# Combining C and B before the transposition, with wider products and a new instruction order, in a state-space convolution kernel

## The chip, the cores and the metric

The kernel runs on one core of one Trainium2 chip. The metric is the device time of one execution in microseconds. The core has five engines, each with its own instruction queue that runs in order: PE (TensorE), DVE (VectorE), ACT (ScalarE), POOL (GpSimd) and SP, which here only issues DMAs. Engines wait for each other through semaphores.

## The reference, cut to what matters

The input `x` has 2048 rows of 512 columns (bf16). Two branches are computed and mixed row by row with a gate `g`:

```
g = sigmoid((x * gate_w).sum(-1))
# branch a: a convolution along the 2048 rows, one kernel K per column d
dt    = exp(log_dt)                                  # 512
P     = exp(dt * A * l)                              # A complex, 512 x 128 states, l = 0..2047
K     = real(sum_n C[d,n] * P[d,n,l] * dt * B[d,n])  # C and B complex
a     = causal_conv(x, K) + x * Dskip                # by FFT in the reference
# branch b: the two rows with the largest x @ w_r go through a gated MLP and are added back
b     = x + scatter(silu(xs @ w_gate) * (xs @ w_up) @ w_down * sigmoid(r))
out   = g * a + (1 - g) * b
```

For this change what counts is `C * dt * B`, a complex product of 512 x 128 numbers that the kernel needs transposed (states on the partitions), and the products of spectra by which the convolution is done.

## The kernel before, in words

**How the order is set.** The kernel records operations (`P.op`) with what they read and write. Nothing is scheduled at run time: a string `ORDER` lists all operations in one sequence, three characters for each, and a string `SECOND` says for operations that two engines could do (`EV`, `SCL`, `LIN` and some others: ACT or DVE) which one does it. `P.fixed` deals the sequence out to the engines' queues, and `P.emit` adds the waits. A wait is needed for results of other engines and, on DVE and ACT, also for results of the engine itself. So a change of any operation comes with a new `ORDER` and `SECOND`, and every queue may be rearranged, SP's queue of DMAs included.

**Helpers and their lines.** Most DVE products come from `TT` (L483, a tensor_tensor), scalings from `TS` (L487) and `SCL` (L502 on either engine), PSUM evictions from `EV` (L498 on either engine), exponentials, sines and tanh on ACT from `AC` (L494). DMAs come from `DMA` (L505).

**Opening.** `PRM` receives A, C and B (real and imaginary part, 512 x 128 each); `CB` receives constants (`c_bf`: first the identity, later the rest). 28 matmuls on dummy data (L617) fill PE while it waits. `ptr` (L628) transposes the six parameter matrices, 24 blocks of 128 x 128, into PSUM. `dtp` spreads log_dt over all partitions and ACT takes its exponential, `DTB`. DVE then forms, with rows put into the order that the tables need: `AL` = dt * Re A, `TMP[0]` = dt * Im A, `TMP[1]` and `TMP[2]` (scaled and rounded, L648), `B16` (L651: the angle in 16 bits), `PBR` = dt * B, `CM1` and `CM2` (C times the two parts of B), and `WW` = C * dt * B.

**Tables.** `exps1` and `exps2` are 26 exponentials of `AL` on ACT. `trig` scales `B16` by a lag (`SCL`, L502), takes the sine, adds a quarter turn (L694) and takes the sine again. `tab1` and `tab2` multiply these into tables `TP` (lags in steps of 8) and `R` (`r00` to `r31`: `WW` times powers), for two halves of the states' columns, h = 0 and 1. Exponentials and sines need different function tables on ACT; a change of table is an `ACT_TABLE_LOAD` (L255).

**Forward, kernel and spectra.** `forward` (L900) transforms the input, in two blocks of 1024 rows and four frequency tiles, with matrices `F` from `c_fwd`; `EV` puts the result into `X`. `kgen` (L917) multiplies tables to give the convolution kernel `KA`; `sel` (L933, L945) picks rows of it for half 0, and for half 1 twenty small DMAs do (`tap`, "AR<-AR" among the DMA issues), into `KC`. `sel3` (L966) picks rows for eight output rows that rounding puts at block edges ("edge rows"). `kspec` (L986, L991) transforms `KC` into spectra `KK`.

**Products and inverse.** `products` multiplies `X` with `KK` on DVE, for half h and block blk; block 1 also needs block 0's input times a second spectrum. `inverse` adds up, in four PSUM banks, the skipped input and the edge rows (L1038, L1039) and the inverse transform (L1051, in groups of 8 or 4 matmuls), evicts with the gate (L1059) and stores to `out`. Block 1 is done ahead of block 0.

**Routing.** Eight DMA transposes of `x` (L762), 64 small matmuls (L771) for gate and routing logits, a search for the two largest, and the MLP (L812, L835, L851). `xed` (L820) picks input rows for the edge rows, out of four tiles of `U` (the input in SBUF). Sixteen scalings of `U` (L880) prepare the mix.

Of the kernel before, what the change touches and what calls it, by code (L numbers as in the profile page):

```python
# [373 lines left out]
ETB = sorted({tok(s)[0] for _, _, src in EROWS for s in src})  # L374
ECOL = 384
# [3 lines left out]
def small_mats():  # L379
    eye = np.eye(128)  # L380
    sgn = np.diag(np.where(np.arange(128) % 2 == 0, 1.0, -1.0))
    xs = np.zeros((128, len(ETB), EW))
    ek = np.zeros((128, 4, 2, EW))
    oh = np.zeros((NE, 16 * 128))
    for r, (t, k, src) in enumerate(EROWS):
        for s in src:
            tb, p = tok(s)
            xs[p, ETB.index(tb), 32 + r] = 1.0
# [4 lines left out]
    return np.concatenate([eye, sgn, -sgn, xs.reshape(128, -1), ek.reshape(128, -1)], 1), oh  # L393
# [3 lines left out]
    "00100300p00q00r00200000700o01401500601700501801c01b01p00402201e00h01d01601i01y01f01k01v01g00g01901q01j01h01x01a00802301u03u04w01n01o03t02s00a04x03v00s"  # L397
    "00t00u00v02002402d01r04303s04404200w00x00y00z01002b01s01t00c02604500901101201l01301w02102702q05903w03x03z04603y02t04704805b04z04y01m05805a04902g04005c"
    "00b02j04f05005105204a04104b05d05f02502m02i05e02u05g05h05302902o02r05502n05402p02v04n01z04e02w02l04c02a00e03304m05s03404d00i02k03502c05t03602f02e04p037"
    "03802h04g05600f02805v04o04q03903a04j05u03b03i05700d04h05w04t04i04r04s04k03d05i05k03j07807907a04l05j05l00n07l03o07s07j07b07c05y00l04u05m07r07i03e03f07t"  # L400
    "07k07m00j07e07h07q07d07u06004v07n05x05z06105n05p07g03g07o05o05q07v06207w03k03l09s06307f07p09t09h06e06f09r07x03m05r06h03n03q09u09v06g09i06506407y06609w"
    "06i06709x09j07z08108006j08309k06k06m0680820ae08508409l06906l06n08609m09o06b06a06c06d09n08908b0ad08a08e08f0a408h06z09y08c0a308808706y07003p06o08d0a1071"
    "07200k08g08i08j0ac09p0a20a508k08l08m08o08n08q0ab09z0af0a808p06q08s08r0a609q0a70a006p0a900m06r0am0al0ag08t0aa0an08u0ao07408w0b80ai0ah0ay0ax0az0ap0b508v"
    "0aj0b708y08x0aw0900b60ak08z0920au0aq0ar0at03r02x07306s06u0b00b306w0av0b90b106t0ba0bb0bc0as0be0bh0bd0b20b40bf0760bg0bj0bi0750bl0910bk0bu09306v0br09d0bq"
# [19 lines left out]
def bass_gated_mix__ssm_conv_s4__moe_arch_mod__prompt_kernel(nc, A_u, A_A_re, A_A_im, A_B_re, A_B_im, A_C_re, A_C_im, A_log_dt, A_Dskip,  # L424
# [22 lines left out]
    with ExitStack() as es:  # L447
# [640 lines left out]
        for qd in range(2):  # L1088
            products(0, (qd,), (1,), pset=qd)
# [57 lines left out]
```

## Time and profile before

| What | us |
|---|---|
| Median of 3 runs | 169.58 (169.01 to 169.94) |
| Profiled execution, its own time | 168.23 |
| Its span, first to last instruction | 166.4 |
| DVE busy | 152.9 |
| PE busy | 148.1 |
| ACT busy | 117.2 |
| Mean granted clock of TensorE | 0.969 |

The profile is of one execution. A matmul's busy time counts from its start to its modelled end, and matmuls overlap, so PE's busy time is not its work; start-to-start distances are. On DVE and ACT an instruction that waits for nothing starts a little before the end of the one ahead of it, so durations add up to slightly more than the time. A line of a view names the helper's line (L483 for nearly every product), so products are told apart by their shapes. "AR" is the one large SBUF tensor in which all buffers lie, "ps" is PSUM.

### The profile page before, as it was taken

The page shows a single profiled execution, that of the slowest core. Times are in us where ns is not written, and L with a number is a line of the kernel's source. Part 1 is how long each engine was busy: PE and PEld are TensorE (multiplying, and loading weights), DVE is VectorE, ACT ScalarE, POOL GpSimd, SP SyncE. Part 2 cuts the span into 40 slices and gives each one's busy share as a digit, 9 for nine tenths or more (in the row PEclk, how much of TensorE's full clock was granted, in tenths as well). Part 3 has the DMA queues.
Part 4 walks back from the last instruction along what each step waited for, and adds up shares of the span by engine and source line. Part 5 has one row for each costly group of instructions (what it writes and reads, how often), then busy time and mean ns, then how long its engine had stood idle before and what let it go on. Part 6 is the DMA issues. An engine that isn't in the chain of part 4 may idle for free.

```text
span 166.4 us, 3916 instructions
## 1 busy us (share of the span) xinstructions
PE 148.1 (89%) x1644; PEld 101.7 (61%) x1644; DVE 152.9 (92%) x255; ACT 117.2 (70%) x197; POOL 2.8 (2%) x7
## 2 busy tenths in 40 slices
PE   5999959999999998997489999968989999989980
PEld 1644415456364348692257799837857888878860
DVE  1699998899999998999999999999999999999970
ACT  3499999799999999999744777992043658408022
POOL 2000000000000000000000004000000000000000
PEclk9999987999999999999858999999999999999999
DMA  4999998996000000000995502941020000130505
GB/s 151 218 341 203 146 241 290 415 398 267 4 0 0 0 4 0 4 0 7 330 353 196 190 7 61 378 123 26 13 61 8 0 0 0 35 95 0 158 4 160
DMA packets 22584, 20.33 MB, mean 122 GB/s; under 512 B 12187, under 2 KB 19102, under 8 KB 22438
## 3 DMA queue, kind: packets, MB, share of 16 engines
q1 hardware_dynamic: 22276, 19.81, 39.7%
q8 instruction: 13, 0.21, 0.5%
q10 hardware_dynamic: 290, 0.26, 0.5%
q14 instruction: 5, 0.04, 0.1%
HBM read 15.54 MB, written 2.10 MB: 106 GB/s over the span
## 4 chain that ended last, share of the span: by engine, by line
DVE 52%; ACT 28%; PE 9%; issue 6%; DMA 2%; SPq 0%; DVEq 0%
DVE AR L483 44%; ACT AR L494 13%; ACT AR L498 7%; ACT AR L502 4%; PE ps L900 3%; ACT AR L694 3%; DVE AR L498 2%; PE ps L1051 2%; PE ps L628 2%; DVE AR L502 2%; DMA AR<-c_bf 2%; DVE AR L880 1%; PE ps L917 1%; PE ps L771 1%; DVE AR L1059 1%
## 5 line engine op out<-in xcount | busy, mean ns | idle before, releaser
L483 DVE TENSOR_TENSOR AR<-AR 128x1024 bf16<-128x1024 bf16 (+8 forms) x151 | 119.9, 839 | 1.3
L498 ACT ACTIVATE AR<-ps 128x512 bf16<-128x512 f32 (+7 forms) x71 | 45.0, 667 | 17.9 <-PE ps L986 10.2
L900 PE MATMUL ps<-AR 128*128 128x512 bf16 x192 | 45.5, 390 | 2.4 <-DVE AR L498 2.1
L494 ACT ACTIVATE AR<-AR 128x512 bf16<-128x512 f32 (+4 forms) x56 | 41.4, 791 | 2.6 <-DVE AR L483 2.2
L900 PEld LDWEIGHTS ps<-AR 128*128 128x128 bf16 x192 | 18.1, 100 | 25.4 <-DVE AR L498 2.6
L1051 PE MATMUL ps<-AR 128*128 128x256 bf16 x256 | 30.4, 273 | 1.3 <-DVE AR L483 1.3
L1051 PEld LDWEIGHTS ps<-AR 128*128 128x128 bf16 x256 | 24.8, 98 | 5.1 <-DVE AR L483 1.9
L1059 ACT ACTIVATE AR<-ps,AR 128x256 bf16<-128x256 f32 x25 | 10.8, 474 | 21.9 <-PE ps L1051 21.7
L986 PE MATMUL ps<-AR 128*128 128x256 bf16 x160 | 21.0, 282 | 0.3 <-issue 0.3
L917 PEld LDWEIGHTS ps<-AR 128*128 128x128 bf16 x512 | 18.8, 98 | 2.1 <-ACT AR L498 0.7
L917 PE MATMUL ps<-AR 128*128 128x84 bf16 (+1 forms) x512 | 19.4, 199 | 0.5 <-ACT AR L498 0.4
L986 PEld LDWEIGHTS ps<-AR 128*128 128x128 bf16 x160 | 15.5, 101 | 4.5 <-issue 0.7
L502 DVE TENSOR_SCALAR AR<-AR 128x256 int32<-128x256 f32 (+1 forms) x39 | 11.4, 325 | 0.6 <-ACT AR L494 0.6
L502 ACT ACTIVATE AR<-AR 128x256 int32<-128x256 f32 (+1 forms) x25 | 10.0, 437 | 0.0
L617 PE MATMUL ps<-AR 128*128 128x512 bf16 x28 | 8.3, 462 | 1.5 <-DVE AR L612 1.5
L1038 PE MATMUL ps<-AR 128*128 128x256 bf16 x32 | 7.7, 274 | 2.1 <-DVE AR L498 1.4
L1039 PE MATMUL ps<-AR 128*128 128x256 bf16 x32 | 7.6, 273 | 0.0
L483 DVE TENSOR_TENSOR AR<-AR,ps 128x256 f32<-128x256 bf16 (+2 forms) x6 | 3.4, 627 | 4.1 <-PE ps L628 4.1
L617 PEld LDWEIGHTS ps<-AR 128*128 128x128 bf16 x28 | 3.0, 112 | 5.4 <-issue 1.9
L991 PE MATMUL ps<-AR 128*128 128x512 bf16 x16 | 5.6, 380 | 0.1
L694 DVE TENSOR_SCALAR AR<-AR 128x1024 int32<-128x1024 int32 (+1 forms) x9 | 5.7, 629 | 0.0
L1038 PEld LDWEIGHTS ps<-AR 128*128 128x128 bf16 x32 | 3.1, 97 | 3.6 <-DVE AR L498 1.5
(66 smaller groups left out, 81.6 us busy)
## 6 DMA issues: line engine op xcount, KB each, us to landing
AR<-c_ksp SPq DMA_DIRECT2D x5, 512.0 KB, 5.5
AR<-c_inv SPq DMA_DIRECT2D x1, 2048.0 KB, 8.0
out_dram<-AR SPq DMA_DIRECT2D x16, 128.0 KB, 2.2
AR<-in_B_w_gate_dram SPq DMA_DIRECT2D x1, 1792.0 KB, 12.8
AR<-in_B_w_up_dram SPq DMA_DIRECT2D x2, 896.0 KB, 10.9
AR<-c_fwd SPq DMA_DIRECT2D x3, 512.0 KB, 6.9
AR<-in_A_u_dram SPq DMA_DIRECT2D x2, 512.0 KB, 5.3
AR<-in_A_u_dram SPq DMA_DIRECT2D x1, 1024.0 KB, 7.7
```

Of the source, the lines that this page charges most:

```text
L483: return P.op(DVE, lambda h: h.tensor_tensor(out=o, in0=a, in1=b, op=op), rd, wr, cost=tt_cost(o, a, b), **k)
L494: return P.op(ACT, lambda h: h.activation(out=o, in_=a, func=func, scale=scale, bias=bias), rd, wr, cost=0.185 + nel(o) * 0.833e-3 + (0.09 ...
L498: return P.op((ACT, DVE), (lambda h: h.activation(out=o, in_=a, func=ACTF.Copy), lambda h: h.tensor_copy(o, a)), rd, wr, cost=(0.185 + n * ...
L502: return P.op((ACT, DVE), (lambda h: h.activation(out=o, in_=a, func=ACTF.Copy, scale=c), lambda h: h.tensor_scalar(out=o, in0=a, scalar1= ...
L617: last = h.matmul(fwp[1](0, 128, k * 512, (1, D)), DUM(0, 128, 0, (1, 128)), DUM(0, 128, 0, (1, D)), start=True, stop=True)
L694: P.op((DVE, ACT), (lambda hh: hh.tensor_scalar(out=w, in0=w, scalar1=16384.0, scalar2=None, op0=ALU.add), lambda hh: hh.activation(out=w, ...
L900: last = h.matmul(o, w, U2(0, 128, st * D, (1, D)) if pm else U(0, 128, (blk * 8 + st * 2 + par) * D, (1, D)), start=(pm + par + st == 0), ...
L917: last = hh.matmul(pb(0, 128, (g - b0) * W4 + o, (1, n)), TP[h][1 - i // 2](0, 128, g * 128, (1, 128)), r[i](0, 128, g * n, (1, n)), start ...
L986: last = hh.matmul(pb(0, 128, n * 256, (1, 256)), KP[u](0, 128, (tau + n) * 128, (1, 128)), KC[h](0, 128, jg * 256, (1, 256)), start=(k == ...
L1038: hh.matmul(pb(0, 128, e * 256, (1, 256)), IDN(0, (1, 128)), U(0, 128, tb[e] * D + h * HC, (1, HC)), start=(e == 0), stop=False)
L1051: last = hh.matmul(pb(0, 128, e * 256, (1, 256)), G(0, 128, ((par * 2 + part) * 4 + ft) * 512 + (2 * t2 + e) * 128, (1, 128)), X(0, 128, h ...
L1059: P.op((ACT, DVE), (lambda hh, o=o, i_=i_, g_=g_: hh.activation(out=o, in_=i_, func=ACTF.Copy, scale=g_), lambda hh, o=o, i_=i_, g_=g_: hh ...
```

## The change

1. **Opening.** C is multiplied with both parts of B ahead of the transposition, packed and in bf16 (`PAB`, two products of 1024). `pwr` then transposes and adds up in one: for each of eight blocks two matmuls against the identity, the second with a negated identity (`NID`) where the complex product needs a minus, summed in PSUM (`psw`). `WW` is then one product with dt. A is transposed by matmuls against an identity whose columns are read in the tables' order and whose result is written in that order (`ptr`: runs of four floats at steps of 16), so that `AL` is one plain product and `TMP[1]` comes out of one scalar_tensor_tensor; `TMP[0]`, `PBR`, `CM1` and `CM2` are gone.
2. **Products.** For half 0, block 1, the first products are still made by pairs of frequency tiles; all that follow are done for the four tiles at once.
3. **Edge rows.** Six rows of the input are loaded by two small DMAs into `XSR`, and `xed` is one matmul on six rows.
4. **Coefficient DMAs (`tap`).** Every other one is issued from ACT.
5. **Stores by bank.** A store covers the two row tiles of one PSUM bank instead of the two parities of one row tile; there are still 16.
6. **A new `ORDER` and `SECOND`.** All 26 exponentials now stand ahead of the first sine on ACT. On SP the order of the opening loads, and of the transposes among them, is another; the rest of `c_bf` goes out ahead of the gate weights.

The diff, cut to its core (shortened expressions end in `..`):

```diff
@@ opening @@
-        pps = [misb[0], misb[1], kgb[0]]
-        for q in range(3):
+        idp = lambda b, *c: b(0, 128, *c, (64, 2), (1, 16), (16, 4))
+        pto = lambda b, c, k: b(0, 128, c + 4 * k, (HC, 2), (16, 16), (1, 4))
+        psa = [kgp[0], kgp[1]]
+        for q in range(2):
             def ptr(h, q=q):
-                for i in range(2):
-                    for k in range(4):
-                        last = h.transpose(pps[q](..), PRM(..), IDN(0, (1, 128)))
+                for k in range(4):
+                    last = h.matmul(pto(psa[q], 0, k), PRM(..), idp(CB, 0), start=True, stop=True)
+        for q in range(2):
+            TT(PAB(0, 128, q * 1024, (D, 2), (1, D)), PRM(0, 128, 2 * D, ..), PRM(0, 128, (4 + q) * D, ..), ALU.mult, ..)
+        for part in range(2):
+            def pwr(h, part=part):
+                for k in range(4):
+                    h.matmul(pto(psw, part * D, k), PAB(..), idp(CB, 0), start=True, stop=False)
+                    last = h.matmul(pto(psw, part * D, k), PAB(..), idp(CB, 0) if part else idp(NID, 0), start=False, stop=True)
...
-        for h_ in range(2):
-            TT(prd(AL, 0, h_), nat(DTB, 0, h_), tra(pps[0], 0, h_), ALU.mult, ..)
-        for h_ in range(2):
-            TT(prd(TMP[0], 0, h_), nat(DTB, 0, h_), tra(pps[0], D, h_), ALU.mult, ..)
+        TT(f512(AL), f512(DTB), psa[0](0, 128, 0, (1, D)), ALU.mult, ..)
-        LIN(f512(TMP[1]), f512(TMP[0]), [TMP[0]], [TMP[1]], scale=-c16)
+        STT(f512(TMP[1]), psa[1](0, 128, 0, (1, D)), -c16, f512(DTB), ALU.mult, ALU.mult, ..)
...
-        TT(PBR(..), DTB(..), pps[2](..), ALU.mult, ..)
-        TT(c2(CM1), pps[1](..), PBR(..), ALU.mult, ..)
-        TT(c2(CM2), pps[1](..), PBR(..), ALU.mult, ..)
-        for h_ in range(2):
-            TT(prd(WW, 0, h_), tra(CM1, 0, h_), tra(CM2, D, h_), ALU.subtract, ..)
-            TT(prd(WW, D, h_), tra(CM1, D, h_), tra(CM2, 0, h_), ALU.add, ..)
+        TT(WW(0, 128, 0, (D, 2), (1, D)), DTB(0, 128, 0, (0, 2), (1, D)), psw(..), ALU.mult, ..)
@@ edge rows @@
+            for t0 in (0, BLK):
+                DMA([(XSR(ESRC.index(t0), len(ts), 0, (1, D)), dr(A_u, t0 * D, ..))], [], [(XSR, t0)], 4096)
-                for i, tb in enumerate(ETB):
-                    last = h.matmul(xe(0, EW, 0, (1, D)), CB(..), U(0, 128, tb * D, (1, D)), ..)
+                return h.matmul(xe(0, EW, 0, (1, D)), CB(0, len(ESRC), ECOL, (1, EW)), XSR(0, len(ESRC), 0, (1, D)), ..)
@@ tap @@
-                    DMA(.., 60000 * nu, prio=1e5, each=0.6)
+                    DMA(.., 60000 * nu, prio=1e5, each=0.6, eng=(SP, ACT)[c4 % 2])
@@ products @@
+            if blks == (1,) and len(fts) == 4:
+                for qd in qds:
+                    xq = X(0, 128, h * 8192 + 4096 + 512 * qd, (2048, 2), (1024, 2), (1, 512))
+                    for P_, part in ((PA, 0), (PBb, 1)):
+                        kq = KK[h](0, 128, part * 2048 + 512 * qd, (0, 2), (1024, 2), (1, 512))
+                        TT(P_(0, 128, 512 * qd, (2048, 2), (1024, 2), (1, 512)), xq, kq, MUL, ..)
             for blk in blks:
-                for P_, part in ((PA, 0), (PBb, 1)):
+                for P_, part in ((PA, 0), (PBb, 1)) if blk == 0 or len(fts) < 4 else ():
                     TT(v4(P_), xv(blk), kv(0, part), MUL, ..)
@@ inverse @@
-                for st in range(4):
-                    tb = blk * 8 + st * 2
-                    DMA([(dr(out, (1024 * blk + 256 * st) * D + h * HC, (2 * D, 128), (D, 2), (1, HC)), U(..))], ..)
+                for t2 in range(2):
+                    for par in range(2):
+                        tb = tbs(t2, par)
+                        DMA([(dr(out, (1024 * blk + 512 * t2 + par) * D + h * HC, (2 * D, 128), (256 * D, 2), (1, HC)), U(..))], ..)
@@ calls @@
-        for qd in range(2):
-            products(0, (qd,), (1,), pset=qd)
+        products(0, (0, 1), (1,))
```

More of the change, by code (lines that the diff above doesn't have):

```diff
@@ L373 @@
 NE = len(EROWS)
-ETB = sorted({tok(s)[0] for _, _, src in EROWS for s in src})
+ESRC = sorted({s for _, _, src in EROWS for s in src})
 ECOL = 384
@@ L399 @@
[L399 to L402, printed above, removed]
```

104 lines of the change are left out of this document (55 added, 49 removed).

## The prediction

> **What bounds the kernel now.** I read first the page's busy times, then the windows by stage, the groups of VectorE by shape, the chain of waits, and the timeline of the opening and of the coefficient DMAs.
>
> The page and the windows (columns: stretch, length, busy us and instructions of PE, PEld, DVE, ACT, POOL, clock, DMA share, GB/s):
>
> ```profile
> PE 148.1 (89%) x1644; PEld 101.7 (61%) x1644; DVE 152.9 (92%) x255; ACT 117.2 (70%) x197; POOL 2.8 (2%) x7
> ```
> ```profile
> 5.57:31.00 25.43, 23.36 (x159) 11.41 (x160) 24.21 (x47) 22.85 (x39) 0.00 (x0) 0.93 1.05 256
> 31.00:80.00 49.00, 45.93 (x578) 26.95 (x575) 48.19 (x97) 48.85 (x74) 0.00 (x0) 1.00 0.22 80
> ...
> 120.30:159.00 38.70, 36.38 (x317) 29.93 (x314) 38.01 (x49) 17.55 (x37) 0.00 (x0) 1.00 0.13 39
> 159.00:166.40 7.40, 3.23 (x28) 2.66 (x28) 2.08 (x5) 1.90 (x4) 0.00 (x0) 1.00 0.31 90
> ```
>
> From its first product at 5.57 us to 159 VectorE has hardly a hole. From 31 to 80 ScalarE is full as well (48.85 of 49.00): there both set the pace together. After 80 ScalarE has half its time free and VectorE alone carries the chain. The last 7.40 us are a tail: 28 matmuls of the inverse, evictions, the last store.
>
> The prices, from the groups by shape (busy us, mean ns | idle before):
>
> ```profile
> L483 DVE TENSOR_TENSOR AR<-AR 128x2048 bf16<-128x2048 bf16 x48 | 57.5, 1220 | 0.4
> L483 DVE TENSOR_TENSOR AR<-AR 128x1024 bf16<-128x1024 bf16 x44 | 29.2, 687 | 0.4
> L483 DVE TENSOR_TENSOR AR<-AR 128x4096 bf16<-128x4096 bf16 x2 | 4.5, 2285 | 0.0
> L483 DVE TENSOR_TENSOR AR<-ps,AR 128x1024 f32<-128x1024 bf16 x2 | 2.5, 1228 | 0.0
> L483 DVE TENSOR_TENSOR AR<-AR 128x256 bf16<-128x256 f32 x4 | 2.3, 606 | 0.0
> L483 DVE TENSOR_TENSOR AR<-AR,ps 128x256 f32<-128x256 bf16 x4 | 2.1, 591 | 4.1 <-PE ps L628 4.1
> L651 DVE SCALAR_TENSOR_TENSOR AR<-AR 128x512 f32<-128x512 f32 x1 | 0.7, 693 | 0.0
> ```
>
> Doubling 1024 elements to 2048 adds 533 ns, so the fixed part is about 0.15 us. The chain shows what follows a product: 1.24 us and 0.02 of "issue" where the next one reads its result,
>
> ```profile
> 131.30 1.24 DVE AR L483
> 132.54 0.02 issue
> 132.56 1.24 DVE AR L483
> ```
>
> while an independent one starts about 0.085 us before the end of the last (four take 4.63 us in the chain, not 4.88). A wait of VectorE for itself thus costs 0.12 us.
>
> **The change, part by part.** Counts come from the two instruction orders.
>
> *Opening arithmetic, VectorE.* Gone: four 128x256 out of PSUM (591 ns), one and two of 1024 (1223, 1228), four of 256 from float (606), one L648 (429): 8.90 us, less 12 overlaps of 0.085, 7.88. New: AL and TMP[1], 512 floats each (priced as L651, 0.69), WW, 1024 out of PSUM (1.22), two of 1024 (0.687), a negated identity (0.19, between the 172 ns and 290 ns of nearby shapes): 4.17 less 0.51, 3.66. Net **-4.2**.
>
> *Half 0, block 1.* Twelve of 2048 and eight of 1024 become eight of 2048 and four of 4096: 20.14 to 18.90 us, and 8 instructions fewer give back 0.68 of overlap: **-0.6**.
>
> *Waits for itself.* 81 of VectorE's operations wait for an earlier one of its own, 65 after: 16 x 0.12 = **-1.9**.
>
> *Handed to ScalarE by the new order.* Two evictions of 1024 (1.22 and 0.68), three of 256 (0.48), two scalings of U (0.34), three small argument scalings go over; two L694 (0.69) come back for a 0.42: **-3.2** on VectorE, +3.7 on ScalarE.
>
> VectorE's queue: -9.9 us in all, 5.3 of it before its last product of the second half's table (92.9 us now) and 4.6 behind that. ScalarE: -2.6, because all exponentials now stand ahead of the sines (two L255 table loads of 1283 ns gone), +3.7, and ten coefficient DMAs.
>
> What of it lies on the path, stage by stage.
>
> Up to the last sine (now 78.9 us) ScalarE is as full as VectorE. Its queue up to there shrinks by 1.6 us (two loads -2.6, small waits -0.3, moved work +1.3). AL comes out of one instruction instead of two (0.69 for 1.10), less 0.1 because it now waits for the exponential of DTB (-0.3 before the first exponential on ScalarE), and the 1.0 us that the first L255 waited for VectorE's L502 goes with VectorE's shorter queue. So **-2.9**; VectorE's 5.3 allows it. The 13 us of VectorE behind the last sine are the same instructions.
>
> Behind 92.9, VectorE alone: -4.6. But something new is late. In PE's new order the first L986 group of half 1 stands behind the last block 1 group of the inverse. From the last product that this group needs: two inverse groups (8 x 0.109 each), two L1038/L1039 groups (4 x 0.109), one L986 group (8 x 0.109) and 0.16 to the result are 3.6 us, and VectorE has 1.22 + 0.48 + 0.27 us queued meanwhile: a hole of some 2 us, where VectorE now has its wide products of block 0. So **-2.6**.
>
> Tail: 20 matmuls instead of 28 wait for the very last product: 8 x 0.109 = **-0.9**. The last store still follows its last eviction, so storing by bank gives nothing more.
>
> Sum -6.4, before the parts that the trace doesn't price:
>
> - *Matmuls with spread rows* (24 of 128 columns at `ptr` and `pwr`, operand and result in steps, for 24 transposes at 107 ns). Low end: packed and at full clock (L1051 stands 109 apart for 256 columns, so 55 for 128), 24 x -0.052 = -1.2 us. High end from L966: with its operand in steps, eight of 64 columns took 1.14 us at half clock (127 ns start to start), with it packed 0.41 at full clock (29 ns, so 58 at half): 2.2 times. 24 x 0.107 x 1.2 is +3.1 us. Most of them stand among L900 groups that wait for loads anyway, and PE was as slow here before; I take +0.5. The Trainium skill, "PSUM — Partial Sum Buffer", Specifications, says that any non-contiguous access pattern slows matmuls significantly. It gives no factor, and no run here shows a matmul that writes in steps; what it would do is the first rival.
> - *Loads.* The order on SP is new. The second frequency tile of c_fwd (512 KB) goes out behind two transposes of U (1.2 to 3.6 us each on SP), some 3 to 4 us later than now; the first tile and U go out earlier, which gains nothing, since ScalarE is busy with exponentials until 19 us. By the bytes ahead of it and the page's GB/s row it lands at 14.7 us, with the 6.9 of its row at 16 to 17; PE is through with the first tile at about 15. Each us beyond is at most one us of ScalarE's queue, where the forward evictions stand between the sines. Between 0 and +2, I take +0.4. c_bf's rest now goes ahead of the gate weights, not behind them (12.2 us now), so the edge rows (one L820 matmul for four) that now stand ahead of L812 on PE should not stop it; if it did land at 12.2, PE, and with it the forward groups, would stand for 1.7 us.
> - *Coefficient DMAs.* SP issues the 20 in 14.2 us, 0.65 apart; ten on ScalarE are 6.5 us in the queue that also evicts. From 93 to 118.3 ScalarE is busy 16.9 of 25.3, so 8.4 cover them; an eviction behind one is up to 0.65 late. 0 to +2, I take +0.4. That they land sooner saves nothing: the last lands at 118.6 now, its reader starts at 125.2.
>
> In all **-5.1 us**. The profiled execution took 168.23 (span 166.4 and 1.8 around it), 0.8% under the median of 169.58; it would take 163.1, and the median 164.5.
>
> **The rivals.**
>
> *Spread rows are dear (slower).* The result of `ptr` and `pwr` goes to PSUM in runs of four floats, 64 bytes apart; no row shows a matmul that writes so. The chain is: AL, TMP[1] and WW wait for these, and PE's forward groups queue behind `pwr`, whose evictions ScalarE takes in order. It decides from 6.4 / 24 + 0.107 = 0.37 us for each; at 0.5 it is +9.4 against -6.4, 171 to 173 us. Against it: L966's 127 ns for 64 columns make 0.25 for 128. For it speaks the sentence of the Trainium skill above.
>
> *ScalarE and PE eat the second half.* Ten DMAs and the evictions taken over delay L986's results, the hole is 4 us and not 2: 167.2. For it: VectorE waits for 16 evictions of half 1 one by one. Against: ScalarE's 17.55 busy of 38.70 behind 120.
>
> *VectorE's cut comes through whole.* No new hole, and loads on time: -9.9 + 2 is 161.5. Against: ScalarE's full 49 us.
>
> *It evens out.* The saved instructions were under cover of ScalarE up to 80 and of PE behind it (36.38 of 38.70): 169.6.
>
> **How the numbers follow.** Forecast 0.57, ScalarE and PE 0.20, whole cut 0.08, evens out 0.05, spread rows 0.10. A measurement of this kernel can tell about 0.5% from no change, so faster 0.85, same 0.05, slower 0.10. The range leaves out the spread rows, the evening out and half of the whole cut, 0.19 together: 161.6 to 168.4.
>
> **What would show it.** VectorE some 143 us busy with 232 instructions; two table loads; the last sine at about 76 us; the last L483 of the second table at 90; a new hole of VectorE near 120, ended by PE's L983 group; 20 matmuls behind the last product. It would be wrong if `ptr` and `pwr` matmuls stand over 0.3 us apart, if PE's forward groups wait past 18 us for c_fwd, or if VectorE has over 8 us of holes from 5.6 to its last product.

## The result, and the profile after

The changed kernel takes 167.41 us (median of six runs, 167.04 to 168.25) against 169.33 of the kernel before in the same runs: ratio 0.990, 95% interval 0.986 to 0.994. The forecast was 164.5 (161.6 to 168.4). The direction was right; of 5.1 us forecast, 1.9 came. The profiled execution took 167.29 us with a span of 165.7, against 168.23 and 166.4; the one before was a fast one of its kernel, so the two profiles differ by 0.9 us and their spans by 0.7, and it is these 0.7 us that the accounting below takes apart.

Executions of one kernel differ in TensorE's granted clock (0.957 to 0.969 in these six), and the time with it; comparisons leave out those over 1.5% above the kernel's fastest, and where only some of a run's executions count, their number is given.

The page's busy times and the windows by stage (stretch, length, busy us and instructions of PE, PEld, DVE, ACT, POOL, clock, DMA share, GB/s):

```profile
PE 149.3 (90%) x1628; PEld 103.8 (63%) x1642; DVE 145.2 (88%) x232; ACT 118.9 (72%) x204; POOL 2.8 (2%) x7
```
```profile
5.57:31.00 25.43, 25.33 (x112) 11.45 (x113) 21.36 (x43) 22.41 (x37) 0.00 (x0) 1.00 1.06 255
...
120.30:159.00 38.70, 37.60 (x334) 32.25 (x334) 34.09 (x44) 16.62 (x34) 0.00 (x0) 1.00 0.16 43
```

VectorE lost 7.7 us of work and 23 instructions, as forecast in kind. But it now has holes in both halves: 4.1 us up to 31 (1.2 before) and 4.6 behind 120 (0.7 before). PE, on the other hand, is full up to 31: 25.33 of 25.43, 23.36 before.

The accounting that decides starts at 5.57 us (VectorE's first product before; 5.38 after) and is cut at four events: the end of the last sine, of the last product of half 1's tables, of VectorE's last product, and the end of the span. First before, then after:

```profile
5.57:79.91 74.34, 69.29 (x735) 38.36 (x735) 72.33 (x142) 71.61 (x112) 0.00 (x0) 0.98 0.50 140
79.91:92.86 12.95, 10.59 (x104) 6.93 (x104) 12.89 (x20) 7.23 (x13) 0.00 (x0) 0.74 0.75 277
92.86:159.33 66.47, 61.74 (x768) 52.59 (x768) 65.28 (x88) 34.55 (x68) 1.85 (x1) 1.00 0.24 72
159.33:166.40 7.07, 2.95 (x28) 2.40 (x25) 1.75 (x4) 1.90 (x4) 0.00 (x0) 1.00 0.33 94
```
```profile
5.57:79.29 73.72, 70.50 (x762) 39.78 (x770) 67.90 (x137) 70.22 (x115) 0.00 (x0) 1.00 0.58 170
79.29:92.71 13.42, 11.84 (x108) 9.01 (x110) 13.42 (x23) 11.69 (x22) 0.00 (x0) 1.00 0.30 103
92.71:159.94 67.23, 60.74 (x734) 52.09 (x735) 62.06 (x72) 32.45 (x62) 1.81 (x1) 0.92 0.25 73
159.94:165.70 5.76, 2.08 (x20) 1.61 (x17) 0.97 (x2) 2.62 (x6) 0.00 (x0) 0.98 0.32 91
```

| Stretch | forecast | measured | VectorE busy | VectorE idle |
|---|---|---|---|---|
| to the last sine | -2.9, and +0.9 unpriced | -0.6 | -4.4 | +3.8 |
| to half 1's last table product | 0 | +0.5 | +0.5 | 0 |
| to VectorE's last product | -2.6, and +0.4 unpriced | +0.8 | -3.2 | +4.0 |
| tail | -0.9 | -1.3 | | |
| sum | -5.1 | -0.7 | | |

Only the tail kept its promise. In the two long stretches VectorE did 7.6 us less, and waited 7.8 us longer. Two questions follow: who paces the opening, and who makes the late hole. In the opening the waits are these, from ScalarE's timeline (start, busy, and in brackets the idle time before it and what ended it):

```profile
24.84 1.06 ACT L493 ACTIVATE AR<-AR 128x1024 bf16<-128x1024 int16 x1 [1.80 <-DVE AR L695]
...
28.43 1.02 ACT L497 ACTIVATE AR<-ps 128x1024 bf16<-128x1024 f32 x1 [0.67 <-PE ps L902]
```

L695, for which ScalarE waits 1.80 us, stands in VectorE's queue behind two waits for PE:

```profile
20.65 1.22 DVE L482 TENSOR_TENSOR AR<-AR,ps 128x1024 bf16<-128x1024 bf16 x1 [0.55 <-PE ps L641]
22.38 1.23 DVE L497 CAST AR<-ps 128x1024 bf16<-128x1024 f32 x1 [0.51 <-PE ps L902]
...
24.12 0.69 DVE L695 TENSOR_SCALAR AR<-AR 128x1024 int32<-128x1024 int32 x1
```

And from PE's timeline up to 31.8 us (the last matmuls of `pwr`, the forward groups, the first 30 of the 64 matmuls of the routing logits):

```profile
20.00 0.40 PE L640 MATMUL ps<-AR 128*128 128x128 bf16 x1
20.22 0.40 PE L641 MATMUL ps<-AR 128*128 128x128 bf16 x1
20.44 10.97 PE L902 MATMUL ps<-AR 128*128 128x512 bf16 x49
31.25 0.89 PE L776 MATMUL ps<-AR 128*128 128x2 bf16 x30
```

A `pwr` matmul starts 0.22 us behind the one before, and PE goes from there to 31.25 without a break; the logits stood at 27.76 before. VectorE's longest hole of the opening is another one: 2.66 us up to 8.72, for the second transposition of A, which stands in PE's queue behind six dummy matmuls (5.09 to 7.62). In the run e15 below it is still 2.21 us, and VectorE waits for PE no more between 12 and 31 us. So it is not what the two waits at 20 to 22 come from: without it VectorE would come to them earlier and wait longer there. No run takes it away.

The late hole, from VectorE's timeline:

```profile
124.61 0.48 DVE L1067 TENSOR_SCALAR AR<-ps,AR 128x256 bf16<-128x256 f32 x1 [1.20 <-ACT AR L1067]
125.00 0.27 DVE L482 TENSOR_TENSOR AR<-AR 1x256 bf16<-1x256 bf16 x1
128.03 0.69 DVE L497 CAST AR<-ps 128x512 bf16<-128x512 f32 x1 [2.75 <-PE ps L988]
128.90 0.69 DVE L497 CAST AR<-ps 128x512 bf16<-128x512 f32 x1 [0.18 <-PE ps L988]
```

1.20, 2.75 and 0.18, with 0.26 at 103.97, are 4.4 us. Ahead of it PE stood for some 5 us between 104 and 112: for a small eviction (of `yt`, a step of the MLP) behind two DMAs in ScalarE's queue, for a result of ScalarE, and for the load `c_oh` (the one-hot rows), issued at 104.51 and landed at 111.86. The chain that ended last in this profile goes through that load. The small eviction, then PE:

```profile
105.82 0.18 ACT L497 ACTIVATE AR<-ps 128x8 bf16<-128x8 f32 x1 [1.47 <-issue]
```
```profile
106.05 0.41 PE L968 MATMUL ps<-AR 128*40 128x64 bf16 x8 [2.06 <-ACT AR L497]
107.96 2.15 PE L876 MATMUL ps<-AR 128*2 128x128 bf16 x16 [1.18 <-ACT AR L865]
111.99 0.37 PE L1046 MATMUL ps<-AR 128*128 128x256 bf16 x1 [1.89 <-DMA AR<-c_oh]
```

Behind these waits PE ran at half clock. The windows of 3.41 us from 103.97 on, and the first two of them before:

```profile
103.97:107.38 3.41, 0.75 (x13) 0.49 (x12) 3.38 (x2) 1.41 (x4) 0.51 (x1) 1.00 0.82 308
107.38:110.79 3.41, 2.03 (x16) 1.45 (x16) 3.35 (x5) 2.19 (x3) 0.00 (x0) 0.50 0.95 303
110.79:114.20 3.41, 2.21 (x11) 1.62 (x12) 3.34 (x4) 2.20 (x4) 0.00 (x0) 0.50 0.24 36
114.20:117.60 3.40, 3.40 (x18) 2.42 (x17) 3.40 (x2) 0.00 (x0) 0.00 (x0) 0.50 0.00 0
```
```profile
103.97:107.38 3.41, 3.41 (x76) 3.10 (x75) 3.38 (x6) 3.41 (x7) 0.13 (x1) 1.00 0.88 341
107.38:110.79 3.41, 2.82 (x30) 1.59 (x28) 3.38 (x6) 3.41 (x8) 0.00 (x0) 1.00 0.84 263
```

Before, PE was 11.29 of these 13.63 us busy at a clock of 1.00, since groups of half 0's spectra stood between the small steps of the MLP and the one-hot rows. The wide products need all these spectra at once, the new order puts them ahead of `kgen`, and nothing is left to fill PE.

### The profile page after: what moved, and what is told of

Read it like the earlier page. It is cut to its first block, busy times and chain, and to the rows that moved or that the text cites. A ratio compares the mean times of both kernels' runs of the same rounds, so it can differ in the third digit from the quotient of the medians.

```text
span 165.7 us, 3881 instructions
## 1 busy us (share of the span) xinstructions
PE 149.3 (90%) x1628; PEld 103.8 (63%) x1642; DVE 145.2 (88%) x232; ACT 118.9 (72%) x204; POOL 2.8 (2%) x7
## 4 chain that ended last, share of the span: by engine, by line
issue 62%; DVE 16%; PE 13%; DMA 4%; POOLq 1%; ACT 1%; POOL 0%
DVE AR L482 16%; PE ps L1059 8%; DMA AR<-c_oh 4%; PE ps L988 2%; PE ps L1046 2%; PE ps L1047 1%; POOLq L446 1%; ACT AR L1067 1%; ACT AR L497 0%; POOL AR L600 0%; POOL AR L601 0%; POOLq L1140 0%
## 5 line engine op out<-in xcount | busy, mean ns | idle before, releaser
L482 DVE TENSOR_TENSOR AR<-AR 128x1024 bf16<-128x1024 bf16 (+8 forms) x141 | 117.6, 886 | 1.5 <-PE ps L837 0.3
L497 ACT ACTIVATE AR<-ps 128x512 bf16<-128x512 f32 (+5 forms) x73 | 47.2, 680 | 12.0 <-PE ps L988 5.7
L902 PE MATMUL ps<-AR 128*128 128x512 bf16 x182 | 42.7, 379 | 1.3 <-ACT AR L497 0.5
L1059 PE MATMUL ps<-AR 128*128 128x256 bf16 x256 | 31.6, 281 | 1.1 <-DVE AR L482 0.9
L902 PEld LDWEIGHTS ps<-AR 128*128 128x128 bf16 x192 | 17.7, 98 | 21.6 <-ACT AR L497 2.7
L1067 ACT ACTIVATE AR<-ps,AR 128x256 bf16<-128x256 f32 x28 | 12.7, 472 | 25.2 <-PE ps L1059 23.1
L1059 PEld LDWEIGHTS ps<-AR 128*128 128x128 bf16 x256 | 25.6, 101 | 5.9 <-DVE AR L482 2.1
L988 PE MATMUL ps<-AR 128*128 128x256 bf16 x160 | 20.1, 273 | 1.1 <-ACT AR L497 1.0
L919 PEld LDWEIGHTS ps<-AR 128*128 128x128 bf16 x512 | 18.9, 98 | 2.5 <-ACT AR L497 1.4
L988 PEld LDWEIGHTS ps<-AR 128*128 128x128 bf16 x160 | 15.2, 98 | 5.0 <-ACT AR L497 1.7
L501 DVE TENSOR_SCALAR AR<-AR 128x256 int32<-128x256 f32 (+1 forms) x36 | 10.5, 328 | 0.2
L1046 PE MATMUL ps<-AR 128*128 128x256 bf16 x32 | 8.6, 299 | 1.9 <-DMA AR<-c_oh 1.9
L615 PE MATMUL ps<-AR 128*128 128x512 bf16 x28 | 8.9, 468 | 1.4 <-DVE AR L610 1.4
L1047 PE MATMUL ps<-AR 128*128 128x256 bf16 x32 | 8.7, 300 | 0.0
L695 DVE TENSOR_SCALAR AR<-AR 128x1024 int32<-128x1024 int32 (+1 forms) x10 | 6.6, 664 | 0.9 <-ACT AR L493 0.8
L882 ACT ACTIVATE AR<-AR 128x512 bf16<-128x512 bf16 x10 | 6.9, 716 | 0.5 <-issue 0.5
L497 DVE CAST AR<-ps 128x1024 bf16<-128x1024 f32 (+1 forms) x4 | 3.8, 958 | 3.6 <-PE ps L988 2.9
L615 PEld LDWEIGHTS ps<-AR 128*128 128x128 bf16 x28 | 3.0, 113 | 5.2 <-issue 1.7
L482 DVE TENSOR_TENSOR AR<-AR,ps 128x512 f32<-128x512 bf16 (+2 forms) x3 | 2.1, 700 | 4.4 <-PE ps L632 3.9
```

Source lines behind the costliest of these rows:

```text
L482: return P.op(DVE, lambda h: h.tensor_tensor(out=o, in0=a, in1=b, op=op), rd, wr, cost=tt_cost(o, a, b), **k)
L497: return P.op((ACT, DVE), (lambda h: h.activation(out=o, in_=a, func=ACTF.Copy), lambda h: h.tensor_copy(o, a)), rd, wr, cost=(0.185 + n * ...
L501: return P.op((ACT, DVE), (lambda h: h.activation(out=o, in_=a, func=ACTF.Copy, scale=c), lambda h: h.tensor_scalar(out=o, in0=a, scalar1= ...
L615: last = h.matmul(fwp[1](0, 128, k * 512, (1, D)), DUM(0, 128, 0, (1, 128)), DUM(0, 128, 0, (1, D)), start=True, stop=True)
L902: last = h.matmul(o, w, U2(0, 128, st * D, (1, D)) if pm else U(0, 128, (blk * 8 + st * 2 + par) * D, (1, D)), start=(pm + par + st == 0), ...
L919: last = hh.matmul(pb(0, 128, (g - b0) * W4 + o, (1, n)), TP[h][1 - i // 2](0, 128, g * 128, (1, 128)), r[i](0, 128, g * n, (1, n)), start ...
```

## The experiments

The runs are numbered e1 to e18. In kernels with added lines the helpers' lines move by two to ten (L482 is L484 or L486 there).

### First round: one suspect at a time

**Spread operands taken away (e1).** `ptr` and `pwr` read the identity and write PSUM packed.

```
- idp = lambda b, *c: b(0, 128, *c, (64, 2), (1, 16), (16, 4))
+ idp = lambda b, *c: b(0, 128, *c, (1, 128))
- pto = lambda b, c, k: b(0, 128, c + 4 * k, (HC, 2), (16, 16), (1, 4))
+ pto = lambda b, c, k: b(0, 128, c + 128 * k, (1, 128))
```

> The matmuls of ptr and pwr read the identity packed and write PSUM packed (the states and columns then land in another order, so A and C times B do not meet their own dt: that part of the result is left out, the instruction counts are the same). Theory 1 (spread rows are the lost gain of the opening): the 16 matmuls of pwr, 0.22 us apart in the changed kernel (16.07 to 20.22), stand some 0.055 to 0.11 apart; the two holes of VectorE behind PE (0.55 and 0.51 us at 20 to 22) and most of ScalarE's 1.80 at 24.84 go; the last product of the second half's table ends 1.0 to 1.8 us ahead of 92.7; time 165.6 to 166.4. Rival (the forward groups wait for their loads, or ScalarE's queue of exponentials is the bound): PE waits instead, ScalarE's hole stays above 1.2 us, 167.0 to 167.5.

Measured: ratio 0.991 (0.986 to 0.996); six of twelve executions count, and the clocks of all twelve lie between 0.937 and 0.964. In the trace, of an execution of 170.72 us that is not among the six, the matmuls stand 0.055 us apart, and ScalarE's first wait is 0.51 instead of 1.80. But PE now waits 2.7 us for the transposes of x ahead of the logits and falls to half clock behind that. By time the rival is right. By mechanism theory 1 is: the matmuls and the wait behind them shrink as it says, and the gain goes elsewhere.

**Coefficient DMAs back on SP (e2).** `eng=(SP, ACT)[c4 % 2]` is taken out of `tap`.

> All twenty coefficient DMAs on SP again, everything else as changed. Theory 2 (two DMAs on ScalarE ahead of the small eviction of yt make PE wait from 104 to 106, its clock falls to half from 107.4 to 117.6 and the inverse and the spectra of half 1 come late): the eviction of yt follows the down projection by 0.3 us, not 1.9; PE's first wait falls from 2.1 to under 0.7; the half clock is gone or one 3.4-us window shorter; VectorE's hole before 128 us (4.1 us in three pieces) shrinks by 1.5 to 3; time 164.5 to 166.0. Rival (the DMAs on ScalarE are covered, the hole comes from the wide products and the load of c_oh): hole and clock as before, 167.0 to 167.5, or slower if SP issues the last taps after 120 us.

Measured: ratio 0.984 (0.979 to 0.990), but that counts three executions of twelve, with clocks of 0.969 and 0.979 (165.2 to 167.1); the nine others had 0.958 or 0.959 (167.8 to 169.7), so for the time it is inconclusive. The trace is of one of the nine (169.16 us). The waits of PE from 100 to 130 us in it (us in total, times, longest):

```profile
PE ps L876 <- DVE AR L482: 2.5, 1, 2.5
PE ps L1046 <- DMA AR<-c_oh: 1.4, 1, 1.4
PE ps L876 <- ACT AR L865: 0.8, 1, 0.8
PE ps L968 <- ACT AR L497: 0.5, 1, 0.5
```

L968, which waited 2.1 us for the eviction behind two DMAs, waits 0.5; but the second transposition of the one-hot rows (L876) then waits 2.5 for a small product that stands behind two wide ones on VectorE. The half clock and the hole's 2.75 us at L497 stay. So in this execution the ten DMAs on ScalarE are not what makes the hole: the wait they make is replaced by the next one in the same chain. The three faster executions left no trace.

**PE kept busy (e3).** Filler matmuls on constants, 11 behind `dn`, 6 behind its transposition, 12 behind `tro`:

```
+ for q in range(29):
+     P.op(PE, lambda h: h.matmul(fwb[0](0, 128, 0, (1, D)), CB(0, 128, 0, (1, 128)), CB(0, 128, 0, (1, D)), start=True, stop=True), ...)
```

> 29 matmuls of 512 columns on constants into a free PSUM bank are added on PE, 11 behind the down projection, 6 behind the transposition of its result, 12 behind the transpositions of the one-hot rows, so that PE is not idle from 104 to 112 us. Theory 2: the clock stays full from 104 to 118, the inverse of half 0 needs 3 instead of 6 us for its 40 matmuls, PE gets to half 1's spectra 2.5 to 4 us earlier than 125, VectorE's 2.75-us hole at 128 falls under 1; time 164.0 to 165.5, although ScalarE still issues ten DMAs. Rival: the clock does not follow PE's idle time, or the inverse waits for c_oh and VectorE's products anyway: 167.0 to 167.6.

Measured: 166.03 us (165.25 to 167.35), ratio 0.986 (0.981 to 0.991). The three fastest executions, at clocks of 0.996 and 1.000, took 165.25 to 165.42. The clock follows PE's idle time, as theory 2 says: in the trace it stays at 1.00 from 104 to 121 us, where PE is now full. But VectorE's 2.75 us at L499 fall only to 1.92, not under 1; the gain over the changed kernel is 1.4 us by the medians and 0.7 by the ratios (0.990 to 0.986), less than the 1.9 to 3.4 expected.

**Narrow products again (e4)** in half 0's block 1, by pairs of frequency tiles (20 products for 12), in the changed order.

> Half 0, block 1 by pairs of frequency tiles again (20 products for 12), the order otherwise as changed. Rival to theory 2 (the wide products make the hole: all tiles of block 1 come late together, so the inverse starts late): the inverse of block 1 starts 2 us earlier, VectorE's hole before 128 shrinks by 1 to 2 us while its queue grows by 1.3: 166.5 to 167.3. Theory 2: the inverse's first matmuls wait for the half clock and c_oh, not for the products; VectorE is 0.6 to 1.3 us longer busy, the hole takes most of it up: 167.2 to 168.0.

Measured: ratio 1.003 (1.000 to 1.006), slower than either theory has it. The hole stays (1.66, 2.75 and 0.18 us), and PE waits longer still:

```profile
PE ps L876 <- DVE AR L482: 2.3, 1, 2.3
PE ps L968 <- ACT AR L497: 2.0, 1, 2.0
PE ps L876 <- ACT AR L865: 1.2, 1, 1.2
PE ps L1046 <- ACT AR L497: 1.1, 1, 1.1
```

The wide products as such do not make the hole: without them, but in the order made for them, the hole is as long and VectorE's queue longer. The hole comes with that order.

### Second round: which side of the operand, and the clock

Two runs of one execution each, read for the distances of the matmuls alone (e5, then e6):

> ptr and pwr write PSUM packed, the identity is still read in the tables' order (the columns land in another order, which is left uncorrected). If the write in runs of four floats sets the 0.22 us of a matmul, they now stand about 0.06 apart (a packed 128 columns at full clock, half of the 0.109 for 256); if the read of the identity at steps of 16 sets it, they still stand 0.22 apart.

> The identity is read packed, ptr and pwr still write PSUM in runs of four floats, 64 bytes apart (the columns land in another order, uncorrected). If the read sets the 0.22 us, they stand about 0.06 apart; if the write does, 0.22 remains. Values between would share it.

PE's timeline, packed write with the stepped read first, then packed read with the stepped write:

```profile
17.23 0.40 PE L641 MATMUL ps<-AR 128*128 128x128 bf16 x1
17.45 0.40 PE L640 MATMUL ps<-AR 128*128 128x128 bf16 x1
```
```profile
16.02 0.22 PE L641 MATMUL ps<-AR 128*128 128x128 bf16 x1
16.07 0.22 PE L640 MATMUL ps<-AR 128*128 128x128 bf16 x1
```

0.22 against 0.055 us from start to start: the read of the identity at steps of 16 elements (32 bytes) costs four times the packed one, and the write in runs of four floats costs nothing. The prediction's first rival had looked at the write. The Trainium skill, "SBUF — State Buffer", Door 1: The DMA port swizzle, says that SBUF is read in lines of 16 bytes, so that bf16 may be strided up to 8 elements for free: a step of 16 is beyond that, and the trace agrees. (Steps between 1 and 16 no run here shows.) The Trainium skill, "PSUM — Partial Sum Buffer", Specifications, which the prediction cites, says that any non-contiguous pattern slows matmuls significantly: for runs of four floats in PSUM the trace shows no such cost.

Then both kernels with fillers at each one's own long waits of PE, so that the clock is the same (e7, e8):

> The changed kernel with filler matmuls at every wait of PE over 0.6 us between 70 and 120 us (29 as in the filled run, 14 more ahead of the row selections at 76 and 80 us and of the first spectra that wait at 86), so that the granted clock is 1.00 throughout. Theory 2: every run near the lowest of the filled kernel, 165.3 us, spread under 0.5. Rival (the fillers stand in the way of the real matmuls): 166 or more at full clock.

> The kernel before with filler matmuls at its own waits of PE (9 at 23 us, 12, 3 and 3 ahead of the row selections at 80 to 85, 14 between 109 and 125). From its runs (168.0 at a clock of 0.979, 169.5 at 0.959) a full clock is worth 1.4 us: 166.6. Then the change itself is worth 1.3 us at the same clock (165.3), and most of the forecast 5.1 is missing for reasons other than the clock. If the clock took the gain, this kernel is at 167.5 or more and the change is worth over 2.2 us.

Measured: changed 166.18 us (165.63 to 167.30), ratio to the kernel before as it is 0.984 (0.978 to 0.989); kernel before with fillers 167.76 (167.08 to 168.33), 0.993 (0.990 to 0.996). Between the two the ratio is 0.9835 / 0.993 = 0.990, what it is without fillers. Neither has the full clock throughout (two of six executions at 1.000, the others 0.986 to 0.996; five of twelve, the others 0.983 to 0.994), and neither came as low as its expectation; 167.76 even lies where the expectation would have the clock take the gain. What decides is the difference, 1.6 us by the medians, and it is what it was. The clock costs each of them 1.0 to 1.2 us; it explains none of the difference to the forecast, though in the changed kernel's profile it lengthens the hole: at full clock the span is 164.1 and the hole

```profile
126.41 0.69 DVE L499 CAST AR<-ps 128x512 bf16<-128x512 f32 x1 [1.92 <-PE ps L996]
127.28 0.69 DVE L499 CAST AR<-ps 128x512 bf16<-128x512 f32 x1 [0.18 <-PE ps L996]
```

is 2.1 us, and 2.8 with 0.69 at 104. The inverse starts at 112.6 us there, where the fillers end, and not earlier than in the changed kernel (112.0), where it waited for `c_oh`. This kernel, "at full clock", is the base of what follows: near one clock, smaller effects can be seen. The runs were made on different chips, so they are compared by their ratios to the kernel before.

### Third round: the opening

> On the full-clock kernel: the identity in the tables' order is stored packed beside the plain one (128 more columns of c_bf in its first DMA), so that ptr and pwr read it without steps; 8 fillers ahead of the routing logits keep PE busy while the transposes of x land; on VectorE the first quarter turn (L695) goes ahead of an eviction and one product of the second table ahead of the routing chain. Theory 1: ScalarE's waits of 1.74 and 0.67 us (for L695, for a forward group) go; the last sine ends at 77.0 to 77.8 instead of 79.2, the last product of the second half's table at 90.4 to 91.2 instead of 92.65; time 164.0 to 164.9 against 166.2 (median of the full-clock kernel). Rival (the transposes of x, which land at 31 us, are next and hold PE and VectorE up): the last sine stays at 78.5 to 79.2, time 165.5 to 166.3.

> The opening run again, with one more edit: SP issues the five transposes of x that stood behind the second half of the input and the last forward matrices ahead of these. In the opening run ScalarE was 2.2 us ahead at 25 us and 0.6 behind at 44: the routing logits wait for the transposes, and the small products of the gate, whose results stand in ScalarE's and VectorE's queues, for the logits. Theory 1b (the new order on SP, which lets the last transpose land at 31 us, is the floor under the opening): the logits start at 28 to 29 us instead of 31, the last sine ends at 77 to 78, the last product of the second half's table at 90.5 to 91.5 (92.65 at full clock without these edits, 93.2 in the opening run); time 164.0 to 165.0 against 165.6 of the opening run. Rival (the DMA queues are full until 40 us in any order, something else lands late instead: the last forward matrix or the gate weights): the last sine stays at 78.8 to 79.8, 165.3 to 166.5.

The packed read without a change of the result: the identity is stored a second time with its columns in the tables' order,

```
+ prm = eye[:, 64 * (n // 64) + n % 64 // 4 + 16 * (n % 4)]
- return np.concatenate([eye, sgn, ...
+ return np.concatenate([eye, prm, sgn, ...
```

and in the second run SP's five late transposes of x are issued ahead of the last forward matrices. Measured: 165.56 us, 0.981 (0.976 to 0.985), in e9, and 165.66, 0.982 (0.977 to 0.988), in e12. Both theories missed: the last sine ends at 79.8 and 79.4, no earlier than 79.2 at full clock, and where the transposes land makes no difference between these two. PE's waits from 11 to 46 us in the second run name the reason:

```profile
PE ps L908 <- DVE AR L501: 1.1, 1, 1.1
PE ps L908 <- DMA AR<-c_fwd: 0.9, 1, 0.9
```

My own edits had loaded PE: 8 fillers ahead of the logits are 1.7 us in its queue, and an eviction that I had moved back on VectorE holds a forward group up. If that decides, PE is the pace, and the next run, with the two helpful edits alone, should gain.

> The full-clock kernel with the packed identity in the tables' order and the transposes of x ahead on SP, but without the 8 fillers ahead of the logits and without the reordering on VectorE, which in e9 and e12 put 1.7 and 1.1 to 1.8 us onto PE (fillers, and a forward group that waits for the eviction that was moved back). Theory 1c (PE, without a gap from 12.6 to 46 us in the changed kernel, paces the opening; each us off its queue there moves the tables): the logits start near 28.5 instead of 31.25, the small products of the gate end by 40.5 instead of 42.4, the last sine ends at 77.2 to 78.2, the last product of the second half's table at 90.6 to 91.6, time 164.2 to 165.2 against 166.2. Rival (PE is not the pace, or the loads are the floor): PE waits for loads instead, last sine 78.8 to 79.5, 165.6 to 166.4.

Measured (e15): 163.39 us (162.69 to 163.97), ratio 0.970 (0.965 to 0.974) against 0.984 without the two edits, which is 2.4 us. The logits stand at 28.90 and the last sine ends at 76.95, both 2.3 us earlier, as the span is (161.8 for 164.1). PE, and the last three sines on ScalarE:

```profile
17.50 11.56 PE L906 MATMUL ps<-AR 128*128 128x512 bf16 x50
28.90 1.74 PE L780 MATMUL ps<-AR 128*128 128x2 bf16 x64
```
```profile
73.99 2.96 ACT L497 ACTIVATE AR<-AR 128x1024 bf16<-128x1024 int16 x3
```

It was more than theory 1c asked for. Which of the two edits it was:

> e15 without its edit on SP: the packed identity alone on the full-clock kernel. PE is through with the forward groups ahead of the logits at 28.9 us, but the last transpose lands at 31: PE waits some 1.7 us (as in e6), may fall to half clock for a window behind that, and keeps at most 0.6 of the 2.3 us of e15's span: 165.4 to 166.4. If the transposes were not needed early, it would be as fast as e15 (163.4).

> e15 without the packed identity: the transposes ahead on SP alone. PE's queue, with the spread operand in it, reaches the logits at 31 us in any case, so earlier transposes gain nothing and the later forward matrices may cost a little: 165.8 to 166.8. If loads were the pace of the opening, it would gain 1 us or more: 165.2 or less.

Measured: packed identity alone (e17) 166.14 us (164.01 to 167.80; four of six executions count, 0.982, 0.975 to 0.990), new place of the transposes alone (e18) 165.78 (0.985, 0.979 to 0.991, against 0.984 of the base). Alone, neither moves the median. With the first alone PE waits for the transposes and then runs at half clock (0.50 from 33.6 to 37.0 us), here in an execution of 167.28 us:

```profile
31.13 1.84 PE L780 MATMUL ps<-AR 128*128 128x2 bf16 x64 [2.57 <-DMA AR<-in_A_u_dram]
```

With the second alone PE comes to the logits at 31.44, as its queue has it. The spread read and the late transposes hid each other: both end at 31 us, and the 2.3 us came, run by run, only with both edits. How late transposes cost their time is less clear. The one execution of e17 that kept the full clock took 164.01 us, with a span of 162.5: 1.6 us under the base's 164.1, and 0.7 over e15. So much of the price seems to be the half clock behind PE's wait, and not the wait; that execution left no trace.

### Fourth round: the hole

On the full-clock kernel, the last four of ScalarE's coefficient DMAs go to SP and the first spectra of half 1 ahead in PE's queue; in the second of these runs all eight groups of the first frequency pair, and two gated evictions of VectorE behind its next products.

> On the full-clock kernel: the last four of ScalarE's coefficient DMAs, which stand there behind gated evictions of the inverse (117.4 to 119.3), are issued by SP; the addition that completes the coefficients goes ahead of two products on VectorE, and the first four spectra groups of half 1 ahead of two inverse groups on PE. Theory (the hole of 2.1 us at 124 to 127 comes from the late coefficients and from the place of the spectra behind the inverse in PE's queue): the hole falls under 0.6, time 164.2 to 164.9 against 166.2. Rival (the spectra's evictions or the inverse of block 0 become late instead): the hole moves to behind 130, 165.6 to 166.4.

> The full-clock kernel with the edits of the hole run, and beyond them: all eight spectra groups of half 1's first frequency pair go ahead of the last inverse groups of block 0 and of two row groups on PE, and the two gated evictions on which VectorE waited 1.65 and 0.94 us in the hole run go behind its first products of half 1. Theory: with neither the coefficients nor PE's queue late, VectorE goes from half 0's last product (123.8) to half 1's first within 0.5 us, its holes from 120 to 135 fall from 2.1 (full-clock kernel) and 3.1 (hole run) under 0.8, time 164.4 to 165.2 against 166.2. Rival (PE is full from 112 to 130 at full clock, and what is put ahead there pushes other work onto the path): 165.8 to 167.

Measured: 166.91 us, 0.988 (0.984 to 0.992), in e10, slower than its base (0.984, 0.978 to 0.989); and 165.08, 0.979 (0.972 to 0.985), in e14, faster. Both intervals overlap the base's; the spans of the profiled executions, 165.0 and 163.6 for 164.1, go the same ways. In the first the hole moved, as its rival says, and the time is over both ranges: VectorE got to the spectra at 123.3 and then stood 1.65 and 0.94 us for evictions in its own queue. In the second VectorE goes from half 0 to half 1 without a break, and has one wait later, of 1.51 us where under 0.8 was expected:

```profile
124.67 1.29 DVE L499 CAST AR<-ps 128x512 bf16<-128x512 f32 x2
...
134.18 5.91 DVE L484 TENSOR_TENSOR AR<-AR 128x2048 bf16<-128x2048 bf16 x6 [1.51 <-ACT AR L499]
```

So the hole is made by the order, besides the clock: another order of the same work, with four DMAs moved, closes it. Late coefficients, the spectra's place in PE's queue and gated evictions in VectorE's were changed together, and what each is worth was not tested.

> The kernel of e12 with the second half's edits of e14 as well. If the opening's gain and the hole are independent: e12 and e14 add up, 162.5 to 164.0. If not, no better than the better one.

> The opening's and the hole's edits together, at full clock. If the two losses are independent, the sum: 162.2 to 163.4. If one covers the other (VectorE's earlier tables only lengthen the wait for the coefficients, whose DMAs start behind the last kgen group): no better than the better one of the two, 164 to 165.

With the openings that gained little (e13, then e11): 164.76 us, 0.977 (0.971 to 0.983), for the second edits of the hole, which is what the two parts give in sum (0.982 and 0.979, from a base of 0.984); 166.95, 0.990 (0.983 to 0.996; five of six executions count), for the first edits, no better than either part. Both miss their expected times. For e13 it is the parts that had missed theirs, and the sum holds; why e11 falls short of its sum (0.985) was not followed up.

> The kernel of e15 with the edits of the second hole run (165.1 by itself). If the two gains are independent: 163.0 to 164.2; if not, 164.5 to 165.2.

Measured (e16): 162.63 us (161.66 to 163.01), ratio 0.964 (0.959 to 0.969), 0.8 us under e15, which was measured together with it. Opening and hole are nearly independent (-1.4% and -0.5% of 0.984, in sum 0.965). It does all that the changed kernel does, and beats the kernel before by 3.6% and the changed one by some 2.6% (0.964 / 0.990).

## Why the prediction was right and wrong, step by step

**Right: the direction, and what VectorE is spared.** 232 instructions, two table loads, 20 matmuls behind the last product were as said. VectorE's busy time fell by 7.7 us; the arithmetic, the wide products and the work handed to ScalarE were to give 4.2 + 0.6 + 3.2 = 8.0. It is 145.2 us for "some 143": the -1.9 for VectorE's waits for itself is about what is missing, and no run tests that term. The tail gave 1.3 us for 0.9. No `pwr` matmul stands over 0.3 us apart and no forward group waits for c_fwd past 18 us. Of the signs that would prove it wrong the third came: VectorE has 11.0 us of holes up to its last product, for "over 8" (3.3 before). The last sine starts at 78.3 us instead of 76 (78.9 before), and half 1's tables end at 92.7 instead of 90. (One rival's own sum gives another figure: the whole cut is 169.58 - 7.9 = 161.7, not 161.5.)

**The step that failed first: "Most of them stand among L900 groups that wait for loads anyway, and PE was as slow here before; I take +0.5".** Neither reason held. The forward groups wait for no load: PE has no gap from 12.6 to 31.25 us. And before, PE did its 24 transposes by 7.6 us and ran dummy matmuls until the first forward group at 13.9, and it still had 2.06 us of idle time behind that; the 16 matmuls of `pwr` stand at 16 to 20.4 us, between forward groups. With 4.4 us taken off VectorE, PE became the pace, and its time, harmless before, came onto the path: in e7's profile the chain that ended last stays on PE from 1.45 to 28.4 us. The price itself was near the prediction's high end: 0.22 us apiece for 2.2 x 0.107 = 0.235, and against the transposes 24 x (0.22 - 0.107) = +2.7 for +3.1. On the path are the 16 of `pwr`, 16 x 0.165 = 2.6 us more than packed, of which e15 wins 2.3 back. The rival built on these matmuls looked for their price in the write to PSUM, while it is the read of the identity; it forecast a slower kernel from 0.37 us apiece, and at 0.22 it is no more than a term of the sum.

**With it the step "up to the last sine: -2.9".** It counted ScalarE's queue, whose busy time shrank by 1.4 us, as forecast (2.6 for the loads less 1.3 of moved work). It did not ask who feeds ScalarE's evictions and sines. Its idle time up to the last sine, forecast to fall by 1.6, rose by 0.8, for the 1.80 and 0.67 us shown above. That the term "loads" (+0.4) hid a floor of its own, at the transposes and not at c_fwd, which the prediction named, showed only when the first floor was away (e1, e17).

**The second step: "a hole of some 2 us".** It was 4.4. The hole was placed rightly (near 120, ended by PE's spectra) and counted from the PE queue behind the last block 1 product. Not counted was that PE comes to this queue late: the order takes its filling work away from 104 to 112, and then the clock halves. At full clock the hole is 2.8. The rival "ScalarE and PE eat the second half" named 4 us and 167.2, close to what came. But the ten DMAs on ScalarE that it names do not make the hole by themselves: with all of them on SP it stays in e2's trace. VectorE's cut behind 92.9 came out smaller too: busy time fell by 3.2 and small gaps by 0.4, for the 4.6 forecast.

**Left out: the clock.** The prediction took it as it was. It cost both kernels about the same (1.0 to 1.2 us), so it did no harm to the difference, by luck: the half-clock stretches before (behind 23 and 81 us) went away and a new one came at 107.

**Still open.** The 0.5 us between the last sine and the last table product (three VectorE instructions more, by the new order) were not tested, nor was an earlier load of `c_oh`, nor which of the edits in e14 closes the late hole, nor what late transposes cost at full clock. The rule by which the clock falls is known only from the windows below.

## What to carry to other kernels

When work is taken off the engine that sets the pace, write down next to it which engine's queue has no gap left in that stretch, with its slow instructions priced in full: that one is the pace afterwards. A new order must be read for what it takes away as cover, for each engine's small dependent steps, not only for what it makes late. And two floors at the same time hide each other: a cure that gains nothing alone may be half of one.

## What the runs showed of the hardware

- A matmul of 128 columns that reads its moving bf16 operand at steps of 16 elements starts 0.22 us apart at full clock, for 0.055 packed; writing PSUM in runs of four floats, 64 bytes apart, makes no difference (0.055).
- TensorE's clock fell to half after windows of 3.41 us in which PE was busy 0.75 us (after, 103.97), 0.79 and 1.35 (before, 78.15 and 20.13). It stayed full after windows with 1.94 (before, 108.87) and 2.06 (after, 73.25), and at half clock it stayed half with 2.14 (before, 81.56), 2.03 and 2.21 (after, 107.38 and 110.79) and came back after windows of 3.28 and more. The windows are laid so that the clock changes at their edges. The Trainium skill, "TensorE: Matmul & The Clock Gate", What's actually happening, has the window's 3.4 us, and lets the clock fall after an idle window; here it fell after windows that were 22 to 40% busy.
- A small DMA issued by ScalarE holds its queue for 0.61 to 0.70 us, and an eviction of 0.18 us behind two of them came 1.47 us late.
